# Reading a stored spectrum back in two loads per chunk instead of three (long convolution by FFT, then a phase MLP)

## The chip, the cores and the metric

One core of one Trainium2 chip runs the kernel. The metric is the device time of one execution in microseconds (us). Three runs of the kernel before gave 2083.17, 2084.01 and 2089.09 us; their median is 2084.01 us.

## What is computed

The reference has two parts. The change lies in the first.

```
Xf = rfft(x, n=2*S, axis=1);  Hf = rfft(h, n=2*S, axis=0)
y  = irfft(Xf * Hf, n=2*S, axis=1)[:, :S, :]        # x: 8 x 5696 x 128, h: 5696 x 128
theta = y @ w_theta;  zr, zi = y*cos(theta), y*sin(theta)
u = y + (w_tok_r @ zr + w_tok_i @ zi)               # over the 5696 tokens
out = u + relu(u @ w_ch)
```

The product `Xf * Hf` is complex: it needs, beside each part of x's spectrum, both the real and the imaginary part of h's.

## The kernel before, in words

**The transform.** A transform of length 11392 is cut into 178 x 64. Stage a (`stage_a`, matmuls L248) transforms along 178, of which the 90 frequencies 0 to 89 are kept; stage b (`stage_b`, whose matmuls are those of `f2`, L268) transforms along 64 and multiplies by h's spectrum; stages c (`stage_c`, L439 and L440) and d (`stage_d`, L475) go back. The work on x is cut into 8 groups: 4 pairs of batches times 2 halves of the 128 channels. A group passes all four stages.

**Stage b.** The 90 frequencies are walked in 12 chunks: 11 of 8 and a last one of 2. For a chunk, TensorE writes 64 real rows over 64 imaginary rows of x's spectrum into PSUM, ScalarE copies them to `xs` (L417; two buffers), and VectorE multiplies `xs` by both forms of h's spectrum in one instruction of 128 x 2048 (L419; the short last chunk takes two small ones, L424). The products go to `uv_t`, which stage c reads.

**The tile `hs`.** It holds, in 128 partitions, two rows of 512 f16 numbers (1 KB) each. Row 0 is "straight": the real part in partitions 0 to 63, the imaginary part in 64 to 127. Row 1 is "swapped": the imaginary part in 0 to 63, the real part in 64 to 127. There are four `hs` buffers (pool `fft_h`, L112). `load(c)` (L404 to L410) fills one: a load of 128 partitions for the straight row (L408), and two of 64 partitions for the swapped row (L410). Chunk c, once written down, calls `load(c + 4)` (L427), so a buffer that chunk c's multiply frees is refilled for chunk c + 4. Chunks 0 to 3 of the next group are loaded beside stage c.

**Where h's spectrum comes from.** At the start, h itself passes stages a and b. `h_chunk(c)` (L349) puts a chunk's result into the memory of `uv_t` (the views `hst`), and after every third chunk one store of 128 partitions (L362) writes three chunks to the HBM tensor `hf_hbm`. Four stores write all of it. The first multiply of group 0 writes to `uv_t` too, so it has to come after the stores have read their part of it.

**What sets the order.** VectorE, ScalarE and GpSimd (POOL) keep the order in which the code was written, by hand, until group 0 has passed stage c. The order on TensorE and on SyncE's queue (SP), which issues the stores L362 and the loads L408 and L410, is made by a planner. Each queue works in order: what waits at its head holds up what is behind. In one group's time, stage c of group g is woven with stage a of group g + 1 (L778), and then stage b of group g + 1 with stage d of group g (L786). Stage d evicts to `yt` by VectorE (L479) or ScalarE (L481), and at its end SP stores `yt` (L488). The inputs x of group g + 2 are fetched by POOL (L151) beside stage c. After the eight groups come the phases (sine and cosine) and the large product with `w_tok_r` and `w_tok_i` (L1187, L1266).

The pool's buffers serve for something else later: `phases_b` takes `hs` buffers in turn with others for its result `zz` (L582, L583).

Of the kernel before, what the change touches and what calls it, by code (L numbers as in the profile page):

```python
# [11 lines left out]
BF16 = mybir.dt.bfloat16  # L12
F16 = mybir.dt.float16
# [9 lines left out]
def kernel(  # L23
# [10 lines left out]
    nc = tc.nc  # L34
    B, S, D = x.shape
    assert D == 128
    P = 128
# [38 lines left out]
    N2 = 64  # L76
# [3 lines left out]
    CK = 8  # L80
    HD = D // 2
# [6 lines left out]
    NCK = len(CHK)  # L88
# [5 lines left out]
    RC = 2 * NP + 2 * ND  # L94
    M0, N0 = S // 4 // N2, S // 4 % N2
    assert S % 4 == 0 and S // 2 == NB // 2 * N2 + N2 // 2 and 2 * NP < N2 // 2
    hf_hbm = nc.dram_tensor("hf_hbm", (NCK, 2, P, HD * CK), F16, kind="Internal").ap()
    yt_hbm = nc.dram_tensor("yt_hbm", (D, B, S), BF16, kind="Internal").ap()

    psp = ExitStack()  # L100
# [2 lines left out]
    def psum():  # L103
        return fp.tile([P, 2, 512], F32, tag="ps", name="ps")

    conv, setup, xa, xin, pha = (ExitStack() for _ in range(5))

    def pool(name, bufs, stack, **kw):
        return stack.enter_context(tc.tile_pool(name=name, bufs=bufs, **kw))

    fa = pool("fft_a", 1, xa)
    fh = pool("fft_h", 4, xa)  # L112
    fx = pool("fft_x", 2, xin)
    NE, WB, BT = 9, 6 * 4 * CJ * 64, 7 * 1024
    keep = pool("keep", 1, ctx, side="right")
# [172 lines left out]
    hst = [t[:, :6 * D * CK].rearrange("p (c h d k) -> p c h d k", c=6, h=2, k=CK) for t in (u_t, v_t)]  # L288
# [60 lines left out]
    def h_chunk(c):  # L349
        c0, ck = CHK[c]  # L350
        ps = f2(a_h, c, 0)
        h_ = hst[c // 6][:, c % 6]
        dst = h_[:, :, :, :ck]
        if c in (0, 2, 5, 7, 10):
            nc.vector.tensor_scalar(dst, ps, 16.0 / NF, None, op0=mult)
        else:
            nc.scalar.activation(dst, ps, AF.Copy, scale=16.0 / NF)
        for cc, j in ((0, 0), (NCK - 1, CHK[-1][1] - 1)):
            if c == cc:
                nc.vector.tensor_scalar(dst[:, :, :, j], dst[:, :, :, j], 0.5, None, op0=mult)  # L360
        if c % 3 == 2:
            nc.sync.dma_start(  # L362
                hf_hbm[c - 2:c + 1].rearrange("c h p n -> p (c h) n"),
                hst[c // 6][:, c % 6 - 2:c % 6 + 1].rearrange("p c h d k -> p (c h) (d k)"))

    r_u = fc.tile([P, P], F16)
    r_v = fc.tile([P, RC], F16)
# [27 lines left out]
    def e_minus():  # L395
        nc.gpsimd.tensor_scalar(e_neg[:K1], e_t[:K1, 1:2 * NP:2], -1.0, None, op0=mult)

    LEAD = 4

    def stage_b(a_st, dh, warm=WARM):  # L400

        hs_of = {}

        def load(c):  # L404
            if c >= NCK:
                return
            hs = hs_of[c] = fh.tile([P, 2, HD * CK], F16, tag="hs", name="hs")
            nc.sync.dma_start(hs[:, 0], hf_hbm[c, dh])  # L408
            for e in range(2):
                nc.sync.dma_start(hs[64 * e:64 * e + 64, 1], hf_hbm[c, dh, 64 - 64 * e:128 - 64 * e])  # L410

        def chunk(c):
            c0, ck = CHK[c]
            hv = hs_of[c].rearrange("p r (d k) -> p r d k", k=CK)
            ps = f2(a_st, c, warm)
            xs = fs.tile([P, 2, HD, CK], F16, tag="xs", name="xs")
            nc.scalar.activation(xs[:, :, :, :ck], ps, AF.Copy)  # L417
            if ck == CK:
                nc.vector.tensor_tensor(  # L419
                    uv[:, :, :, c0:c0 + ck],  # L420
                    xs.rearrange("p e d k -> p e (d k)").unsqueeze(1).to_broadcast([P, 2, 2, HD * CK]),
                    hv.rearrange("p r d k -> p r (d k)").unsqueeze(2).to_broadcast([P, 2, 2, HD * CK]), op=mult)
            for r in range(2 if ck < CK else 0):
                nc.vector.tensor_tensor(  # L424
                    uv[:, 2 * r:2 * r + 2, :, c0:c0 + ck], xs[:, :, :, :ck],
                    hv[:, r:r + 1, :, :ck].to_broadcast([P, 2, HD, ck]), op=mult)
            load(c + LEAD)  # L427
        return [lambda c=c: load(c) for c in range(LEAD)], [lambda c=c: chunk(c) for c in range(NCK)]

# [63 lines left out]
    zz_n, ZB = [0], 3  # L493
# [11 lines left out]
    rr = []  # L505
    r_rest = [lambda: rr.extend([r_table(0, r_u), r_table(1, r_v)]), lambda: rr[0](), lambda: rr[1]()]
    h_chunk(0)
    w2_sine()
    w_rest(1)
    h_chunk(1)  # L510
    w2_cosine()
    for c in range(2, NCK):
# [24 lines left out]
    def phases_b(ti, y_ap, b0, nb, yT, sb, th_pool, th_tag, zi_eng, turns=None, tags=("red", "mag"), m=P,  # L537
                 theta_ps=None, copy=None, home={}):
        n = nb * D
        if theta_ps is None:  # L540
            theta_ps = th_pool.tile([P, n], F32, tag=th_tag, name="theta_ps")
        theta_ps = theta_ps[:m]
        y_ap = y_ap[:m]
        if tags is None:
            sin_, cos_ = (sb.tile([P, n], F16, tag=t, name=t)[:m] for t in ("sin", "cos"))
        else:
            red, mag = (sb.tile([P, n], F32, tag=t, name=t_)[:m] for t, t_ in zip(tags, ("red", "mag")))
            sin_, cos_ = (z.bitcast(F16)[:, :n] for z in (red, mag))
        if turns is None:
            for b in range(nb):  # L550
                nc.tensor.matmul(theta_ps[:, b * D:(b + 1) * D], yT[:, b, :],  # L551
                                 w_theta_sb, start=True, stop=True)
            nc.scalar.activation(red, theta_ps, AF.Identity, bias=magic[:m])  # L553
            nc.scalar.activation(mag, theta_ps, AF.Copy)
            nc.vector.scalar_tensor_tensor(red, red, MAGIC, mag,
                                           op0=ALU.subtract, op1=ALU.subtract)
            r = red
        else:
            mag = theta_ps
            ones, plus, minus, w_neg = turns  # L560
            for q in range(0, nb, 4):
                bank = theta_ps[:, q * D:(q + 4) * D]
                nc.tensor.matmul(bank, ones, plus, start=True, stop=False)
                for b in range(q, q + 4):
                    nc.tensor.matmul(theta_ps[:, b * D:(b + 1) * D], yT[:, b, :],
                                     w_theta_sb, start=False, stop=False)
                nc.tensor.matmul(bank, ones, minus, start=False, stop=False)
                for b in range(q, q + 4):
                    nc.tensor.matmul(theta_ps[:, b * D:(b + 1) * D], yT[:, b, :],
                                     w_neg, start=False, stop=(b == q + 3))  # L570
            r = theta_ps
        if copy is not None:
            copy()
        if turns is None:
            nc.scalar.activation(mag, r, AF.Abs)
        nc.scalar.activation(sin_, r, AF.Sin, bias=zero_b[:m], scale=-TWO_PI)
        if turns is not None:
            nc.scalar.activation(mag, r, AF.Abs)
        nc.scalar.activation(cos_, mag, AF.Sin, bias=half_pi[:m], scale=-TWO_PI)
        yflat = y_ap.rearrange("p b d -> p (b d)")  # L580
        if tags is None:
            k = zz_n[0] = (zz_n[0] + 1) % (4 + ZB)  # L582
            zz = (fh.tile([P, 2, HD * CK], F16, tag="hs", name="zz").bitcast(BF16) if k < 4 else  # L583
                  sides["phases"]["zz"].tile([P, 2, 512], BF16, tag="zz", name="zz"))
            zr, zi = zz[:, 0], zz[:, 1]
            sides["zz"] = zz
        else:
            zi, zr = (z.bitcast(BF16) for z in (sin_, cos_))
        zi_eng.tensor_mul(zi, sin_, yflat)
        nc.vector.tensor_mul(zr, cos_, yflat)  # L590
        cols = slice(b0 * D, b0 * D + n)
        q_ = b0 // 4
        for e in range((m + 63) // 64):
            rows = slice(e * 64, e * 64 + 64)
            if ti * P >= 2 * H:
                for r, z in enumerate((zr, zi)):
                    nc.sync.dma_start(zl_hbm[r, :, cols], z)
                continue
            p_, blk = divmod(2 * ti + e, 4 * NJ)
            i, j = divmod(blk, NJ)  # L600
            if tags is None and j in home:
                for r in range(2):
                    (nc.gpsimd if r else nc.sync).dma_start(
                        home[j][32 * i:32 * i + 32, :4096].rearrange("p (z q r n) -> p z q r n", z=2, q=2, r=2)[:, :, q_, r],
                        zz[e * 64 + r:e * 64 + 64:2])
            elif tags is None:
                nc.sync.dma_start(z_hbm[p_, j, q_, :, i].rearrange("z t n -> t z n"), zz[rows])
            else:
                for r, z in enumerate((zr, zi)):
                    nc.sync.dma_start(z_hbm[p_, j, q_, r, i], z[rows])  # L610
# [486 lines left out]
    for i, (k, p, tt, j0, s0, nj) in enumerate(stretches):  # L1097
# [38 lines left out]
        if tt is None:  # L1136
# [24 lines left out]
            if end_of_pair:  # L1161
# [5 lines left out]
                c, c0 = c_last  # L1167
# [161 lines left out]
```

## Time and profile before

| what | value |
|---|---|
| median of three runs | 2084.01 us |
| the profiled execution, its own time | 2084.83 us |
| its span, first to last instruction | 2083.0 us |
| TensorE busy (PE) | 1982.1 us, 95% |
| VectorE busy (DVE) | 1543.9 us, 74% |
| ScalarE busy (ACT) | 639.5 us, 31% |
| GpSimd busy (POOL) | 972.4 us, 47% |
| mean granted TensorE clock | 0.978 |
| multiplies L419: count, busy, mean | 88, 111.6 us, 1292 ns |
| loads of `hs`: 128 KB, 64 KB | 96 and 192 |
| stage b, first to last `hs` multiply of group 0 | 53.2 to 72.9 us |
| stage b, first to last `hs` multiply of group 7 | 356.1 to 379.0 us |

How to read it: PE is the matmuls, DVE is VectorE, ACT is ScalarE, SPq is SyncE's queue, where a row is the issue of one DMA. A line number such as L419 is the line of the kernel before. In the view of groups, a row gives busy time and mean duration, and behind the second bar the time that the engine sat idle just before these instructions, and what ended most of it. In the timeline, a row gives start and duration in us, and in brackets the idle time before it and what ended that. "Landing" is the time from a DMA's issue until its data is there.

### The profile page before, as it was taken

The numbers are of one execution on the slowest core, as the hardware profiler recorded it, in microseconds if no ns is written. First come the engines' busy times: TensorE is split into PE (matmuls) and PEld (weight loads), VectorE is DVE, ScalarE is ACT, GpSimd is POOL, SyncE is SP. The second block draws the span as 40 slices with busy tenths as digits, with TensorE's granted clock in tenths as the row PEclk, the third lists the DMA queues.
The fourth block names the chain that finished last, engine by engine and source line by source line (L and its number), as shares of the span: only waits on it lengthen the run. The fifth ranks groups of instructions, "written<-read, shape, count | busy, mean of one in ns | idle before, by whom it ended". The sixth has DMA issues, their size and how long they took to land.

```text
span 2083.0 us, 42942 instructions
## 1 busy us (share of the span) xinstructions
PE 1982.1 (95%) x16381; PEld 1098.0 (53%) x16381; DVE 1543.9 (74%) x2805; ACT 639.5 (31%) x936; POOL 972.4 (47%) x1770
## 2 busy tenths in 40 slices
PE   7698988889999999999999999899999999999998
PEld 5588888754444444444444444344444444444444
DVE  7867767666788787878777766876867777777767
ACT  6667777783333333333310000011111111111111
POOL 8432331247444454445566554445453545444450
PEclk9789999999999999999999999999999999999999
DMA  9699996999898999999999899879697878878793
GB/s 162 97 140 146 157 143 161 240 266 244 147 172 173 178 172 164 175 178 172 179 168 161 131 196 263 132 118 156 119 160 127 154 133 148 144 135 153 129 155 88
DMA packets 518014, 335.08 MB, mean 161 GB/s; under 512 B 186231, under 2 KB 483319, under 8 KB 516823
## 3 DMA queue, kind: packets, MB, share of 16 engines
q0 software_dynamic: 322368, 157.47, 60.0%
q1 hardware_dynamic: 189456, 163.34, 27.7%
q10 hardware_dynamic: 5984, 11.54, 1.6%
q8 instruction: 128, 2.10, 0.4%
q14 instruction: 78, 0.64, 0.1%
HBM read 376.39 MB, written 92.49 MB: 225 GB/s over the span
## 4 chain that ended last, share of the span: by engine, by line
PE 65%; DVE 3%; DMA 3%; issue 1%; POOL 1%; ACT 0%; DVEq 0%; ACTq 0%; SPq 0%
PE m L1266 60%; DVE b L822 1%; DVE c L1273 1%; DMA ring<-in_moe_w_tok_r_dram 1%; PE v L968 1%; PE utp L961 1%; PE m L1270 1%; DMA b<-z_hbm 1%; DVE wt L881 1%; POOL ring L667 1%; PE theta_ps L551 0%; PE tpz L909 0%; DMA wl<-in_moe_w_tok_i_dram 0%; PE m L1187 0%; PE m L1153 0%
## 5 line engine op out<-in xcount | busy, mean ns | idle before, releaser
L667 POOL DMA_DIRECT2D ring<-in_moe_w_tok_i_dram x720 | 387.9, 546 | 651.4 <-DVE wt L881 576.1
L667 POOL DMA_DIRECT2D ring<-in_moe_w_tok_r_dram x720 | 386.5, 547 | 151.0 <-DVE wt L881 82.7
L881 DVE STREAM_TRANSPOSE wt<-ring 128x384 f32<-128x384 f32 (+2 forms) x720 | 360.4, 527 | 120.1 <-PE m L1266 77.5
L1266 PE MATMUL m<-b,wt 128*128 128x512 bf16 x1640 | 390.1, 380 | 1.9 <-DVE wt L881 1.7
L1266 PEld LDWEIGHTS <-wt 128*128 128x128 bf16 x1804 | 176.3, 98 | 219.4 <-DVE wt L881 7.4
L1273 DVE TENSOR_TENSOR c<-c,m 128x512 f32<-128x512 f32 x412 | 266.9, 674 | 0.4 <-PE m L1266 0.4
L963 ACT ACTIVATE ring<-utp 128x512 bf16<-128x512 bf16 x85 | 50.7, 597 | 582.3 <-PE utp L961 582.3
L419 DVE TENSOR_TENSOR uv_t<-xs,hs 128x2048 f16<-128x2048 f16 x88 | 111.6, 1292 | 51.7 <-DMA hs<-hf_hbm 32.4
L439 PE MATMUL ps<-r_u,uv_t 128*128 128x128 f16 x1024 | 123.9, 226 | 16.1 <-DVE uv_t L424 10.9
L440 PE MATMUL ps<-r_v,uv_t 128*128 128x100 f16 x1024 | 121.4, 214 | 1.2 <-DVE uv_t L424 1.0
L1187 PE MATMUL m<-b,wt 128*128 128x512 bf16 x480 | 112.2, 383 | 6.4 <-DMA b<-zz 2.7
L958 ACT ACTIVATE ub<-c 128x512 bf16<-128x512 f32 x88 | 55.0, 628 | 191.8 <-DMA ring<-in_moe_w_tok_r_dram 113.2
L439 PEld LDWEIGHTS <-uv_t 128*128 128x128 f16 x1024 | 104.4, 102 | 12.5 <-DVE uv_t L424 12.1
L151 POOL DMA_DIRECT2D x<-in_x_dram x128 | 99.6, 785 | 22.8 <-POOL x L149 14.7
L440 PEld LDWEIGHTS <-uv_t 128*128 128x128 f16 x1024 | 103.9, 102 | 9.2 <-issue 6.2
L417 ACT ACTIVATE xs<-ps 128x1024 f16<-128x1024 f32 x96 | 91.7, 971 | 48.4 <-DVE uv_t L419 31.6
L1187 PEld LDWEIGHTS <-wt 128*128 128x128 bf16 x528 | 50.9, 99 | 66.4 <-issue 8.7
L268 PEld LDWEIGHTS <-w_t 64*128 64x128 f16 x3240 | 58.3, 99 | 43.8 <-issue 35.7
L553 ACT ACTIVATE red<-theta_ps,magic 128x512 f32<-128x512 f32 (+1 forms) x46 | 31.6, 687 | 155.3 <-PE theta_ps L551 89.4
L248 PE MATMUL ps<-f_t,x 89*128 89x180 f16 x512 | 66.0, 261 | 3.1 <-DVE a L255 1.4
L911 ACT ACTIVATE ring<-tpz 128x512 bf16<-128x512 bf16 (+1 forms) x46 | 27.5, 597 | 131.6 <-PE tpz L909 118.2
L822 DVE TENSOR_TENSOR b<-b 128x1024 bf16<-128x1024 bf16 x100 | 61.4, 684 | 0.0
(2924 smaller groups left out, 3774.6 us busy)
## 6 DMA issues: line engine op xcount, KB each, us to landing
ring<-in_moe_w_tok_r_dram POOLq DMA_DIRECT2D x352, 96.0 KB, 4.5
ring<-in_moe_w_tok_i_dram POOLq DMA_DIRECT2D x352, 96.0 KB, 5.0
ring<-in_moe_w_tok_r_dram POOLq DMA_DIRECT2D x352, 80.0 KB, 4.5
ring<-in_moe_w_tok_i_dram POOLq DMA_DIRECT2D x352, 80.0 KB, 3.9
cp_hbm<-c SPq DMA_DIRECT2D x88, 256.0 KB, 2.5
c<-cp_hbm SPq DMA_DIRECT2D x88, 256.0 KB, 4.3
out_dram<-c SPq DMA_DIRECT2D x88, 256.0 KB, 4.7
hs<-hf_hbm SPq DMA_DIRECT2D x96, 128.0 KB, 3.1
```

Of the source, the lines that this page charges most:

```text
L151: nc.gpsimd.dma_start(x16[p0:p1, e, n0:n0 + 16, :HD], bass.AP(tensor=src.tensor, offset=src.offset + (p0 * N2 + n0) * D + dh * HD, ap=[[N2 ...
L248: nc.tensor.matmul(ps[:, i // 2, (i % 2) * 2 * K1:(i % 2 + 1) * 2 * K1], lhs(q + i), f1_t[:NB], start=True, stop=True)
L417: nc.scalar.activation(xs[:, :, :, :ck], ps, AF.Copy)
L419: nc.vector.tensor_tensor(uv[:, :, :, c0:c0 + ck], xs.rearrange("p e d k -> p e (d k)").unsqueeze(1).to_broadcast([P, 2, 2, HD * CK]), hv. ...
L439: nc.tensor.matmul(o, u_t[:, at:at + P], r_u, start=True, stop=False)
L440: nc.tensor.matmul(o[:, 2 * NP:], v_t[:, at:at + P], r_v, start=False, stop=True)
L667: nc.gpsimd.dma_start(wb[32 * i:32 * i + 32, :ng, :nj * 64], bass.AP(tensor=a.tensor, offset=a.offset + row0 * S + p * H + i * QR + j0 * 6 ...
L822: return [lambda f=f, x=x: f(*x) for f, x in ((nc.vector.tensor_sub, (bt[M3], b12, b22)), (nc.vector.tensor_sub, (bt[M4], b21, b11)), (nc. ...
L881: nc.vector.transpose(wt.rearrange("p j t r -> p (j t r)").bitcast(F32).rearrange("p (j g t) -> p g j t", j=TJ, g=4)[:, :ng, :nj], wb[:, : ...
L1187: nc.tensor.matmul(ms[n // 2 * 2 + h], a[n][:, j, :, r], bts_of[p][jj][n % 2 * 2 + h][:, r, :], start=(n % 2 == 0 and jj == 0 and r == 0), ...
L1266: nc.tensor.matmul(ms[q], a[q][:, j, :, r], bts[jj][q][:, r, :], start=(jj == 0 and r == 0), stop=(jj == NJ - 1 and r == 1 and q not in left))
L1273: nc.vector.tensor_tensor(c, z, ms[q], op=op)
```

## The change

`hf_hbm` gets another shape. Before, a chunk and half of channels had 128 rows of 1 KB: 64 real, 64 imaginary. After, it has 64 rows of 2 KB, in which the real and the imaginary part of a row lie side by side. So partitions 0 to 63 of `hs` (real, imaginary) are one load of 64 rows as they lie, and partitions 64 to 127 (imaginary, real) are one load of the same 64 rows with the two parts in reverse order. A store of 128 partitions becomes two of 64, one for each part. `LEAD`, the number of buffers, stays 4 and only gets its name earlier.

```
-    hf_hbm = nc.dram_tensor("hf_hbm", (NCK, 2, P, HD * CK), F16, kind="Internal").ap()
+    hf_hbm = nc.dram_tensor("hf_hbm", (NCK, 2, N2, 2, HD * CK), F16, kind="Internal").ap()
...
+    LEAD = 4
...
-    fh = pool("fft_h", 4, xa)
+    fh = pool("fft_h", LEAD, xa)
...
-        if c % 3 == 2:
+        for ri in range(2 if c % 3 == 2 else 0):
             nc.sync.dma_start(
-                hf_hbm[c - 2:c + 1].rearrange("c h p n -> p (c h) n"),
-                hst[c // 6][:, c % 6 - 2:c % 6 + 1].rearrange("p c h d k -> p (c h) (d k)"))
+                hf_hbm[c - 2:c + 1, :, :, ri, :].rearrange("c h p n -> p (c h) n"),
+                hst[c // 6][64 * ri:64 * ri + 64, c % 6 - 2:c % 6 + 1].rearrange("p c h d k -> p (c h) (d k)"))
...
-            nc.sync.dma_start(hs[:, 0], hf_hbm[c, dh])
-            for e in range(2):
-                nc.sync.dma_start(hs[64 * e:64 * e + 64, 1], hf_hbm[c, dh, 64 - 64 * e:128 - 64 * e])
+            nc.sync.dma_start(hs[:64], hf_hbm[c, dh])
+            nc.sync.dma_start(hs[64:], hf_hbm[c, dh, :, ::-1, :])
...
-            k = zz_n[0] = (zz_n[0] + 1) % (4 + ZB)
-            zz = (fh.tile([P, 2, HD * CK], F16, tag="hs", name="zz").bitcast(BF16) if k < 4 else
+            k = zz_n[0] = (zz_n[0] + 1) % (LEAD + ZB)
+            zz = (fh.tile([P, 2, HD * CK], F16, tag="hs", name="zz").bitcast(BF16) if k < LEAD else
```

More of the change, by code (lines that the diff above doesn't have):

```diff
@@ L396, in e_minus @@
         nc.gpsimd.tensor_scalar(e_neg[:K1], e_t[:K1, 1:2 * NP:2], -1.0, None, op0=mult)
-    LEAD = 4
     def stage_b(a_st, dh, warm=WARM):
```

## The prediction, made before the changed kernel was run

> **What bounds the kernel now.** The chain of waits, followed back from the end, is TensorE nearly without a gap from about 600 us on; `hs` is not in it. So I read the first 380 us, where `hs` is used: the groups, SP's issues, VectorE's timeline, and the busy time by stage. The row of the multiply, and that of the 128 KB load:
>
> ```profile
> L419 DVE TENSOR_TENSOR uv_t<-xs,hs 128x2048 f16<-128x2048 f16 x88 | 111.6, 1292 | 51.7 <-DMA hs<-hf_hbm 32.4
> hs<-hf_hbm SPq DMA_DIRECT2D x96, 128.0 KB, 3.1
> ```
>
> VectorE sat idle for 51.7 us before L419, by most of it (32.4 us) for `hs`; four waits at L424 make it 34.6 us. Why is the data late, with four buffers? SP's issues in group 2:
>
> ```profile
> 147.09 0.33 SPq L408 DMA_DIRECT2D hs<-hf_hbm  x1
> 147.46 1.08 SPq L410 DMA_DIRECT2D hs<-hf_hbm  x2
> 148.64 0.53 SPq L408 DMA_DIRECT2D hs<-hf_hbm  x1
> 149.22 2.13 SPq L410 DMA_DIRECT2D hs<-hf_hbm  x2
> 151.45 0.53 SPq L408 DMA_DIRECT2D hs<-hf_hbm  x1
> 152.02 1.09 SPq L410 DMA_DIRECT2D hs<-hf_hbm  x2
> ```
>
> SP is never free here: one issue behind another takes 0.585 us, so three take 1.76 us a chunk. A multiply takes 1.226 us (the median of L419). SP, not the wires, is slower than VectorE. VectorE, same group:
>
> ```profile
> 149.11 2.35 DVE L419 TENSOR_TENSOR uv_t<-xs,hs 128x2048 f16<-128x2048 f16 x2
> 153.73 3.60 DVE L419 TENSOR_TENSOR uv_t<-xs,hs 128x2048 f16<-128x2048 f16 x3 [2.27 <-DMA hs<-hf_hbm]
> ...
> 160.16 2.41 DVE L419 TENSOR_TENSOR uv_t<-xs,hs 128x2048 f16<-128x2048 f16 x2 [0.71 <-DMA hs<-hf_hbm]
> 164.11 1.23 DVE L419 TENSOR_TENSOR uv_t<-xs,hs 128x2048 f16<-128x2048 f16 x1 [1.54 <-ACT yt L481]
> ```
>
> Chunk 4 (at 153.73) waits for a load whose last issue ended at 148.54: about 5 us, while x is still being fetched. The last line is chunk 10: its `xs` was done at 162.5 and its load's last issue ended at 161.21, so it too waited for `hs`, though the view names ScalarE. Matching chunks to loads in this way, I also count 2.22 and 1.15 us in group 3 and 0.56 us in group 6. In all the waits for `hs` are, by group 0 to 7: 7.9, 3.4, 4.5, 4.4, 4.5, 6.0, 4.2, 5.0, together 40 us.
>
> Do the stages have room? Busy time by stretch:
>
> ```profile
> 155.00:166.00 11.00, 7.84 (x182) 6.47 (x182) 8.68 (x9) 8.77 (x11) 0.00 (x0) 1.00 0.49 131
> 166.00:187.00 21.00, 20.93 (x388) 20.58 (x389) 14.26 (x12) 14.68 (x19) 9.44 (x18) 0.92 1.31 165
> ```
>
> The columns are the length, then PE, PEld, DVE, ACT and POOL busy, the clock, the DMA share and GB/s. Stage b (first row, its second half) leaves every engine idle at times, the DMA engines half of it. Stage c (second row) is TensorE's. So time won in stage b is won in the whole; time in stage c isn't touched.
>
> **The change, part by part.**
>
> *One issue less per chunk.* The built order of the instructions shows 192 loads instead of 288. On the three compute engines with a kept order nothing moves; TensorE shifts two and three neighbouring pairs. I take 0.585 us for an issue of either new form: 64-row issues of three dimensions (L607) have a median of 0.591 us, 64-row stores (L488) 0.568. Two take 1.17 us, under the multiply's 1.226, so SP stops setting the pace. After an idle SP the last issue of a chunk ends 0.95 us after the buffer is free, not 1.47 (0.33 + 1.08 and the gaps): 0.5 us earlier, and in a full queue another 0.59 us earlier with each chunk.
>
> What is late next: buffer free + 0.95 + landing against three further multiplies, 3.7 us. Late in a stage the data is there about 2.8 us after the last issue ends (161.21 to 164.1): 3.75, a near draw. Early in a stage, with x under way, it is 4 to 5 us, and only 0.5 us is won. So by group what stays is: 0: 1.6 (half of its first wait, below, and 0.5); 1: 2.7; 2 and 3: 1.7 each; 4: 0.7; 5: 1.0; 6: 0.3; 7: 3.6 (two waits beside the large loads of `ya`). Together 13; 27 us of 40 go.
>
> *What then takes the place.* In group 3, TensorE goes from 185.8 to 207.1, 21.3 us, with 18.3 us of work (360 matmuls L268 6.3, L475 8.9, L274 2.1, L248 1.0). It can give 3.0 us at the most, and its order ties it to ScalarE and VectorE. I pass on 0.63 of the 27 us: **17 us**. Bounds of this step: 0 and 40.
>
> *The stores.* Eight issues for four, 4 x 0.59 = 2.3 us more of SP, and they move: the built order has all eight ahead of the first load. Before, loads stood between them, waiting for the first store:
>
> ```profile
> 39.39 0.53 SPq L362 DMA_DIRECT2D hf_hbm<-uv_t  x1
> 39.96 0.55 SPq L408 DMA_DIRECT2D hs<-hf_hbm  x1
> 40.55 2.16 SPq L410 DMA_DIRECT2D hs<-hf_hbm  x2
> 42.81 0.67 SPq L362 DMA_DIRECT2D hf_hbm<-uv_t  x1
> ```
>
> The last store, ready at 37.9, went out at 42.8 and landed 10.2 us later, at 53.0. The first L419 began at 53.19, after 2.26 us idle: it writes the store's source, so this wait was for the store and not for a load. Now that store can go at about 38.5. VectorE's earlier work ends at 50.9, so up to 2.26 us are won. Against it, the stores compete earlier with x, and POOL's tables, for which VectorE waits until 48.27, stand behind x (it waits 1.95 and 2.36 us for landings). I take half, inside the 17. The first loads go about 1 to 2 us later than 37.45; nothing needs them before 50.9, 10 us later, which is their cover.
>
> *The rows.* Bytes stay, 256 KB a chunk. The trace has no load of 64 partitions with 128 KB and none in reverse order, so their landing is open: from 2.0 us (the least of any `hs` load) to 5.6 (`z_hbm<-zz`, the same shape the other way). In group 0 the 64 KB halves landed in 2.3 us, the full 128 KB in 2.4. I take no change; the step's bounds are in the range.
>
> [...]
>
> *The sum.* 2084.83 us (the profiled execution's own time, 0.8 above the median of the runs) less 17 is **2068 us**. Nothing else moves: the pool keeps its four buffers.
>
> **Rivals.**
>
> *Absorbed: 2082 us.* The waits go, but ScalarE's copies and TensorE come late instead. For it: stage b takes VectorE 20.0 to 20.4 us in groups 2, 3, 4 and 6, though their waits as the view names them differ from 1.1 to 4.5. Against it: by my matching the waits are alike (4.2 to 4.5), and the engines have 3 to 4 us idle in each. Only the start and some waits in groups 0 and 5 would be won, about 3 us.
>
> *The clock too: 2060 us.* After each stage b the granted clock drops: 0.72 in 166 to 172, then 1.00; likewise 0.72, 0.78, 0.72 and 0.76 for 6 us after groups 3 to 6. That costs 6 x (0.28 + 0.28 + 0.22 + 0.28 + 0.24) = 7.8 us. TensorE waits 1.4 to 2.6 us for the last multiply at that point, and if that goes, the drops may. [...] Against it: TensorE stays sparse in stage b's end in any case.
>
> *Slower: the reversed half-span load, 2103 us.* The place is the ring of four buffers. A buffer's round is a multiply, two issues and a landing, 1.23 + 0.95 + L, for four chunks. It equals today's 1.76 us a chunk at L = 4.9 us; beyond that the change loses. At L = 6 it is 2.05 a chunk, 0.28 more; with 8 refills in each of 8 groups 64 x 0.28 = 18 us. For it: the early loads already take 4 to 5 us, and a row of the same shape 5.6. Against it: 2.3 us in group 0.
>
> *It doesn't do what it says.* The built order shows it does, so this has no share.
>
> **Chances.** Forecast (10 to 25 us won) 0.50; with the clock 0.14; absorbed 0.20; slower 0.16. Runs of this kernel can tell about 0.3%, 6 us. Most of the absorbed case lies within that, and of the forecast a little: faster 0.67, same 0.18, slower 0.15. The range reaches from 2054, the clock case with the unknown landing at its best, to 2088, over the absorbed case and the mildest slower ones; about 0.1 is left out on each side.
>
> **What would show it.** Right: in stage b SP's issues come in pairs 1.17 us long with gaps between the pairs; the idle time for `hs` before L419 falls from 32.4 to near 13 us; the first L419 begins at 51 to 53 us; stage c's windows stay near 21 us; and group 7's last multiply ends some 17 us before 379. Wrong: a landing of `hs` above 4.9 us at the median; an issue of the reversed load above 1.17 us; or an unchanged stage b with idle time put down to `xs` and TensorE.

## The result, and the profile after

The changed kernel takes 2072.95 us (median of 4 runs, 2070.23 to 2073.84), the kernel before 2086.32 us (4 runs, 2083.17 to 2089.09): a ratio of 0.9934 with a 95% interval of 0.9914 to 0.9955, some 13 us. The forecast was 2068 us. Two later series, each beside runs of the kernel before, gave 0.9938 (0.9922 to 0.9953) and 0.9929 (0.9911 to 0.9946). The profiled execution took 2072.32 us, with a span of 2070.5 us.

First the group rows of the multiplies after the change (L417 was L419, L422 was L424; behind the last bar the idle time of VectorE and who ended it), then the row of the loads:

```profile
L417 DVE TENSOR_TENSOR uv_t<-xs,hs 128x2048 f16<-128x2048 f16 x88 | 110.5, 1290 | 40.7 <-DMA hs<-hf_hbm 22.3 <-ACT xs L415 18.2
L422 DVE TENSOR_TENSOR uv_t<-xs,hs 128x256 f16<-128x256 f16 x16 | 5.9, 410 | 11.0 <-ACT xs L415 10.8
```

```profile
hs<-hf_hbm SPq DMA_DIRECT2D x192, 128.0 KB, 3.6
```

Before, the row of the short last chunk was

```profile
L424 DVE TENSOR_TENSOR uv_t<-xs,hs 128x256 f16<-128x256 f16 x16 | 5.9, 395 | 5.0 <-ACT xs L417 2.8 <-DMA hs<-hf_hbm 2.2
```

The idle time for `hs` before both multiplies fell from 34.6 (32.4 + 2.2) to 22.3 us, not to 13. The wait of the short last chunk for `xs` grew from 2.8 to 10.8 us. SP's issues in group 2, and VectorE beside them:

```profile
144.34 0.45 SPq L407 DMA_DIRECT2D hs<-hf_hbm  x1
144.83 0.60 SPq L408 DMA_DIRECT2D hs<-hf_hbm  x1
...
149.38 0.60 SPq L408 DMA_DIRECT2D hs<-hf_hbm  x1
152.50 0.44 SPq L407 DMA_DIRECT2D hs<-hf_hbm  x1
...
155.55 0.54 SPq L407 DMA_DIRECT2D hs<-hf_hbm  x1
156.13 0.60 SPq L408 DMA_DIRECT2D hs<-hf_hbm  x1
157.00 0.44 SPq L407 DMA_DIRECT2D hs<-hf_hbm  x1
```

```profile
151.24 3.60 DVE L417 TENSOR_TENSOR uv_t<-xs,hs 128x2048 f16<-128x2048 f16 x3 [2.54 <-DMA hs<-hf_hbm]
...
155.76 4.73 DVE L417 TENSOR_TENSOR uv_t<-xs,hs 128x2048 f16<-128x2048 f16 x4
163.53 0.74 DVE L422 TENSOR_TENSOR uv_t<-xs,hs 128x256 f16<-128x256 f16 x2 [3.04 <-ACT xs L415]
```

A pair back to back takes 1.18 us (155.55 to 156.73, and in the median of all), and gaps stand between pairs: SP is idle from 149.98 to 152.50. The late waits for `hs` in this group are gone: four multiplies run without a gap from 155.76. But the fifth chunk, at 151.24, waits 2.54 us, where it waited 2.27 before. Its load's last issue ended at 145.43, 5.8 us earlier. And the last chunk waits 3.04 us for its `xs`. Why, ScalarE's and TensorE's rows tell:

```profile
163.08 0.42 ACT L415 ACTIVATE xs<-ps 128x256 f16<-128x256 f32 x1 [1.98 <-PE ps L275]
```

```profile
160.41 2.63 PE L275 MATMUL ps<-w_t 128*128 128x384 f16 x12
```

L275 are twelve filling matmuls, written before the last chunk's copy into the same PSUM tile and meant only to keep TensorE's clock up. The copy waits for them, 1.98 us. The clock (the figure ahead of the DMA share and the GB/s) in stage b of group 2, then in shorter stretches; the first two rows are the kernel before, its stage b and the first 6 us of the stage c behind it:

```profile
145.84:165.94 20.10, 15.97 (x484) 13.81 (x480) 15.57 (x15) 15.35 (x18) 3.52 (x6) 1.00 0.82 136
166.00:172.00 6.00, 6.00 (x79) 6.00 (x80) 3.64 (x3) 2.32 (x4) 1.11 (x2) 0.72 0.71 174
```

```profile
143.08:164.27 21.19, 18.22 (x484) 15.85 (x480) 15.57 (x15) 14.52 (x17) 3.53 (x6) 0.84 0.82 156
...
153.00:159.00 6.00, 4.72 (x112) 4.52 (x112) 5.97 (x6) 5.27 (x6) 0.00 (x0) 0.64 0.55 159
159.00:164.30 5.30, 5.25 (x53) 3.64 (x50) 2.22 (x4) 2.36 (x5) 0.00 (x0) 0.77 0.65 171
164.30:170.00 5.70, 5.68 (x100) 5.68 (x101) 3.65 (x4) 4.47 (x7) 1.88 (x4) 1.00 0.93 211
```

Before, the clock was 1.00 in this stage b and 0.72 in the first 6 us of the stage c behind it. Now it is low inside stage b, and stage c begins at 1.00. **The drop has moved.**

To add up, I cut the first part of the span at VectorE's timeline: stage b from a group's first to its last `hs` multiply, stage c (with what lies between) from there to the next group's first. "Clock lost" is the sum of (1 - clock) x length over groups 2 to 7. The last two columns are the later series of the changed kernel; of the kernel before there is one profile.

| us | before | after | after, 2nd | after, 3rd |
|---|---|---|---|---|
| first multiply begins | 53.2 | 53.1 | 54.0 | 53.5 |
| 8 stages b | 176.3 | 169.6 | 167.7 | 169.0 |
| 7 stages c | 149.5 | 141.8 | 146.0 | 142.3 |
| last multiply ends | 379.0 | 364.5 | 367.6 | 364.8 |
| from there to the end | 1704.0 | 1706.0 | 1707.0 | 1704.2 |
| clock lost in b | 5.6 | 12.1 | 10.1 | 10.1 |
| clock lost in c | 8.2 | 0.0 | 0.0 | 0.0 |

So the gain has two parts of like size: 6.7 to 8.6 us in stage b, and 3.5 to 7.7 us in stage c. What follows gives 0 to 3 us back; in all the profiles of this study that tail lies between 1702.4 and 1710.8 us, so I read no effect of the change in it.

### The profile page after: what moved, and what is told of

Same layout as the page of the kernel before. It is cut to its first block, busy times and chain, and to the rows that moved or that the text cites. A ratio compares the mean times of both kernels' runs of the same rounds, so it can differ in the third digit from the quotient of the medians.

```text
span 2070.5 us, 42579 instructions
## 1 busy us (share of the span) xinstructions
PE 1969.7 (95%) x16205; PEld 1094.1 (53%) x16381; DVE 1543.0 (75%) x2805; ACT 639.8 (31%) x936; POOL 976.6 (47%) x1770
## 4 chain that ended last, share of the span: by engine, by line
PE 65%; DVE 3%; DMA 3%; issue 1%; POOL 1%; ACT 0%; ACTq 0%; DVEq 0%
PE m L1264 61%; DMA b<-z_hbm 2%; DVE b L820 1%; DVE c L1271 1%; PE v L966 1%; PE utp L959 1%; PE m L1268 1%; POOL ring L665 1%; DVE wt L879 1%; PE theta_ps L549 0%; PE tpz L907 0%; DMA wl<-in_moe_w_tok_i_dram 0%; PE m L1151 0%; PE m L1185 0%; DMA ring<-in_moe_w_tok_i_dram 0%
## 5 line engine op out<-in xcount | busy, mean ns | idle before, releaser
L417 DVE TENSOR_TENSOR uv_t<-xs,hs 128x2048 f16<-128x2048 f16 x88 | 110.5, 1290 | 40.7 <-DMA hs<-hf_hbm 22.3
L437 PE MATMUL ps<-r_u,uv_t 128*128 128x128 f16 x1024 | 116.4, 219 | 5.5 <-ACT g__8966 L442 1.6
L438 PE MATMUL ps<-r_v,uv_t 128*128 128x100 f16 x1024 | 114.0, 207 | 0.4
L415 ACT ACTIVATE xs<-ps 128x1024 f16<-128x1024 f32 x96 | 91.6, 972 | 51.5 <-DVE uv_t L417 26.5
L438 PEld LDWEIGHTS <-uv_t 128*128 128x128 f16 x1024 | 99.9, 98 | 8.4 <-issue 6.5
L437 PEld LDWEIGHTS <-uv_t 128*128 128x128 f16 x1024 | 100.0, 98 | 0.9 <-DVE uv_t L422 0.3
```

The source lines that it names most:

```text
L417: nc.vector.tensor_tensor(uv[:, :, :, c0:c0 + ck], xs.rearrange("p e d k -> p e (d k)").unsqueeze(1).to_broadcast([P, 2, 2, HD * CK]), hv. ...
L437: nc.tensor.matmul(o, u_t[:, at:at + P], r_u, start=True, stop=False)
L438: nc.tensor.matmul(o[:, 2 * NP:], v_t[:, at:at + P], r_v, start=False, stop=True)
```

## The experiments

Theory after the result: SP's work per chunk sets stage b (**A**). Rivals: the landing of half-span loads (**B**); the filling matmuls (**C**); where the clock falls. The kernels ran in three groups, each on one chip, beside runs of the kernel before.

### Three loads again, from the new rows

```
-            nc.sync.dma_start(hs[64:], hf_hbm[c, dh, :, ::-1, :])
+            for r in range(2):
+                nc.sync.dma_start(hs[64:, r], hf_hbm[c, dh, :, 1 - r, :])
```

> The kernel after with the reversed load cut into its two parts, so three issues per chunk again, same bytes, same stores, same tensor in HBM. Theory A (the number of issues on SP sets how late hs is): SP's issues run back to back at 1.76 us a chunk in stage b, the waits of VectorE for hs return to above 30 us, and the time to within 4 us of the kernel before. Theory B (the wider rows or the fewer and larger DMAs land sooner, the issues don't matter): at least two thirds of the gain stay, 9 us or more below the kernel before.

Measured: 2092.87 us (2091.12 to 2100.59), ratio 1.0045 (1.0029 to 1.0061): slower than the kernel before, by 8 us, where theory A allowed 4. Its SP rows in group 2, and its multiply:

```profile
151.26 1.62 SPq L409 DMA_DIRECT2D hs<-hf_hbm  x2
152.98 0.54 SPq L407 DMA_DIRECT2D hs<-hf_hbm  x1
153.57 1.24 SPq L409 DMA_DIRECT2D hs<-hf_hbm  x2
155.08 0.45 SPq L407 DMA_DIRECT2D hs<-hf_hbm  x1
```

```profile
L418 DVE TENSOR_TENSOR uv_t<-xs,hs 128x2048 f16<-128x2048 f16 x88 | 111.9, 1292 | 59.3 <-DMA hs<-hf_hbm 42.2 <-ACT xs L416 16.9
```

SP is full again: a chunk's three issues take 1.83 us (152.98 to 154.81) and more, where they took 1.76 before; all three are now 64-row loads. The waits for `hs` are 43.5 us with L423's, the stages b 184.1. The landing stayed low, 3.2 us for the 128 KB loads and 2.8 for the 64 KB ones, and yet the time was worst. That is for A and against B as the main cause. The clock goes with it: the stages c are back at 151.5 us, with 9.7 us of clock lost in them. The profiled execution was the slowest of the six, 2100.59 us, so its waits and stages are on the high side.

### The old rows, two loads

The kernel before with its four stores and its HBM shape, and two loads that pick the parts out as 1 KB pieces.

```
-            nc.sync.dma_start(hs[:, 0], hf_hbm[c, dh])
-            for e in range(2):
-                nc.sync.dma_start(hs[64 * e:64 * e + 64, 1], hf_hbm[c, dh, 64 - 64 * e:128 - 64 * e])
+            rows = hf_hbm[c, dh].rearrange("(r p) n -> p r n", r=2)
+            nc.sync.dma_start(hs[:64], rows)
+            nc.sync.dma_start(hs[64:], rows[:, ::-1, :])
```

> The kernel before with its tensor and its four stores as they were, and two loads per chunk: each takes 64 rows of two 1 KB pieces, the second with the pieces in reverse order. Theory A: stage b is as in the kernel after; at the start the loads stand between the stores again, as before, and the first multiply waits 2.3 us instead of 3.2; in all 0 to 2 us faster than the kernel after. Theory B (the 2 KB rows side by side matter): the landing rises by 0.5 us or more and the time is 4 us or more above the kernel after.

Measured: 2070.17 us (2065.15 to 2078.07), ratio 0.9934 (0.9916 to 0.9952), the changed kernel's. The gain comes from the count of the loads. The layout in HBM and the eight stores add nothing to it that can be measured, nor do they cost: the first multiply began at 52.8 us here, with four stores, and between 51.5 and 54.0 in the profiles with eight.

### Neither load reversed, and both reversed

```
-            nc.sync.dma_start(hs[64:], hf_hbm[c, dh, :, ::-1, :])
+            nc.sync.dma_start(hs[64:], hf_hbm[c, dh])
```

> The kernel after with the second load in straight order too; partitions 64 to 127 get the real and the imaginary part in the wrong places, so the result isn't the reference's. Theory A: the order of the two 1 KB parts costs nothing, the time is that of the kernel after within 4 us, an issue stays near 0.59 us and the landing near 3.6 us. Rival (the reversed load, with 1 KB pieces, is what lands later than hoped): the landing falls by 0.5 us or more and the time by 5 us or more below the kernel after.

Measured: 2065.23 us (2065.01 to 2066.18), ratio 0.9909 (0.9895 to 0.9923). Pace of a pair 1.17 us, landing 3.5. This is some 4 to 6 us below the changed kernel's three ratios, with intervals that overlap a little. Hence its counterpart, with `::-1` on both:

```
-            nc.sync.dma_start(hs[:64], hf_hbm[c, dh])
+            nc.sync.dma_start(hs[:64], hf_hbm[c, dh, :, ::-1, :])
```

> The changed kernel with both loads in reverse order: partitions 0 to 63 get their two parts in each other's place (the output is another one). The number of issues stays. It doubles the suspected cost of the reverse order, 1 KB pieces in place of 2 KB ones, of which the kernel with neither load reversed showed up to 5 us. If the pieces cost that, 2077 to 2081 us, an issue pair of 1.25 to 1.35 us or a landing above 3.7 us. If not, 2070 to 2076 us, the changed kernel's time.

Beside it ran the changed kernel as it is:

> The changed kernel as it is, beside the others on the same chip: 2070 to 2076 us, ratio 0.993 to 0.995.

Measured: both reversed 2073.81 us (2069.00 to 2075.89), ratio 0.9925 (0.9906 to 0.9944); the changed kernel 2073.53 us (2069.88 to 2076.26), ratio 0.9929 (0.9911 to 0.9946). A second reversed load cost nothing, though the pair took 1.22 us. That alone doesn't clear the first: a chunk waits for the later of its two loads. But the waits for `hs` before the full multiplies are 22.8 us with no load reversed, 24.2 with both, and 21.5 to 26.5 in the three profiles of the changed kernel, so they show no effect of the order. The price of the reverse order is not shown: one pair of kernels has 5 us, the other none. In its profile the kernel without it had stages b of 166.4 us (1.3 to 3.2 below the changed kernel's) and the shortest tail of all, 1702.4 us; that part can have nothing to do with the loads. I leave it open.

### The filling matmuls

The kernel before with 8 more of them in the stages b of groups 1 to 7 (12 to 20), meant to take its clock drops away without touching the loads:

```
-        return (steps, *stage_b(a_st, dh, WARM if g else WARM // 2))
+        return (steps, *stage_b(a_st, dh, WARM + 8 if g else WARM // 2))
```

> The kernel before, loads and all, with 8 more idle matmuls (20 for 12) behind the last chunk of stage b in groups 1 to 7, 1.3 us at the full clock. If the drops of the granted clock at the start of stage c come from TensorE's gap before its first matmul there, they go without any change to the loads: stage c's windows fall from 21.3 to 21.5 us to about 19.9 and the time by 5 to 8 us. If they come from all of stage b's thin second half, the drops stay, and the time is unchanged or up to 9 us longer (7 x 1.3).

Measured: 2085.41 us (2079.90 to 2089.18), ratio 1.0007 (0.9994 to 1.0020). Its stages c fell from 149.5 to 146.0 us, its stages b rose from 176.3 to 179.7. A part of stage c's time is to be had without the loads, but not for nothing. The changed kernel with 6 and with none:

```
+        return (steps, *stage_b(a_st, dh, WARM // 2))
...
+        return (steps, *stage_b(a_st, dh, 0 if g else WARM // 2))
```

> The kernel after with 6 idle matmuls instead of 12 behind the last chunk of stage b in groups 1 to 7. In the kernel after the last chunk's copy to xs waits for these matmuls, since they write the same PSUM tile (waits of 0.8 to 4.1 us before the last multiplies). Theory (what is late next is this fill): the wait before the last multiplies falls by about 1 us in each group, 5 to 8 us faster than the kernel after. Rival (without them the granted clock drops at the start of stage c again): stage c goes back to 21.3 us in most groups and the time is the same or up to 6 us longer.

> The kernel after with no idle matmuls behind the last chunk in groups 1 to 7. Theory (the fill is what is late next, and TensorE is dense enough without it): 8 to 15 us faster than the kernel after. Rival (the clock needs it): stages c of 21 us and more, and a time the same as or longer than with 6.

and, for comparison in the same group, the changed kernel once more:

> The kernel after itself, as the yardstick for the three runs beside it on this chip: 11 to 16 us below the kernel before. Its stage b and stage c lengths also tell which parts of the first profile repeat: if the gain is mostly the clock in stage c, at least five of the six stages c of groups 2 to 7 are again 19.9 us long; if it is mostly stage b, stage b's lengths in groups 3 to 6 are again 1 to 3 us below those of the kernel before.

Measured: with 6, 2076.07 us (2074.10 to 2076.95), ratio 0.9946 (0.9931 to 0.9961); with none, 2067.95 us (2064.17 to 2073.70), ratio 0.9911 (0.9892 to 0.9929); the changed kernel, 2074.86 us (2069.97 to 2076.34). The last chunk's row with none:

```profile
L422 DVE TENSOR_TENSOR uv_t<-xs,hs 128x256 f16<-128x256 f16 x16 | 5.7, 397 | 2.5 <-DMA hs<-hf_hbm 1.6 <-ACT xs L415 1.0
```

The wait for `xs` falls from 10.8 (8.3 in the profile beside it) to 1.0 us, and 6 to 7 us of the time go, by intervals of the ratio that still overlap: three of the six runs took 2064 to 2065 us, the others 2071 to 2074. With 6 matmuls it falls too, to 0.7, and the time does not: a miss. Its stages b of groups 2 to 7 were 4.3 us shorter than the control's, but the profiled tail was 1710.8 us. So C may be a part, of some 6 us, and it isn't a steady one.

### One load per chunk

```
-            nc.sync.dma_start(hs[:64], hf_hbm[c, dh])
-            nc.sync.dma_start(hs[64:], hf_hbm[c, dh, :, ::-1, :])
+            nc.sync.dma_start(hs, hf_hbm[c].rearrange("h p r n -> (h p) r n"))
```

> The kernel after with one load per chunk: 128 rows of 2 KB, 256 KB in one DMA. It takes the rows of both halves of channels instead of the two orders of one, so the result isn't the reference's. SP needs 0.6 us a chunk. If the pace of SP still limits the kernel after, this is 6 us or more faster than it; if what is left is the landing of the early loads beside x and the engines themselves, it is 0 to 5 us faster, and the waits for hs of chunk 4 in groups 2 to 5 are still 0.5 to 2 us.

Measured: 2061.67 us (2057.17 to 2063.14), ratio 0.9882 (0.9863 to 0.9900): 13 us below the changed kernel.

```profile
L416 DVE TENSOR_TENSOR uv_t<-xs,hs 128x2048 f16<-128x2048 f16 x88 | 110.4, 1290 | 30.6 <-ACT xs L414 23.6 <-DMA hs<-hf_hbm 6.8
```

```profile
hs<-hf_hbm SPq DMA_DIRECT2D x96, 256.0 KB, 3.7
```

An issue takes 0.32 us (median), and 256 KB land in 3.7 us, no later than 128 KB did. The waits fall to 6.8 us, the stages b to 158.6 (in the fastest of the four executions, 2057.17 us). Part of the 13 us could lie in the order, since nothing is reversed here either: against the two straight loads, measured on another chip, it is some 6 us by the ratios. The waits for `hs`, 6.8 us against 22.8 with two straight loads, speak for the single load itself. **My view that two issues under the multiply's 1.23 us take SP out of the matter is refuted**: what a chunk needs of SP and of loads still counted.

### One load per chunk, from a second copy

From group 2 on, `hf_hbm` has a second, swapped copy. ScalarE's queue makes it beside stage b of group 1, in 8 DMAs from HBM to HBM.

```
+            if g > 1:
+                nc.sync.dma_start(hs, hf_hbm[c, dh].rearrange("s p r n -> (s p) r n"))
+                return
...
+            copied = nc.scalar.activation(xs[:, :, :, :ck], ps, AF.Copy).ins
+            if g == 1 and c == 1:
+                with tc.issue_after(copied):
+                    for q in range(0, NCK, 3):
+                        for r in range(2):
+                            nc.scalar.dma_start(hf_hbm[q:q + 3, :, 1, :, r].rearrange("c h p n -> p (c h) n"),
+                                                hf_hbm[q:q + 3, :, 0, :, 1 - r].rearrange("c h p n -> p (c h) n"))
```

> The changed kernel, but from group 2 on each chunk comes in one load of 128 partitions. For that a second, swapped copy of h's spectrum is written in HBM by 8 DMAs (3 MB) that ScalarE's queue issues beside stage b of group 1; groups 0 and 1 load as after the change. All that is computed stays. Theory (SP's pace per chunk and not the landing sets stage b): groups 2 to 7 win what the kernel with one wrong load won, 13 us times 6/8, about 9 or 10 us against the changed kernel; from it goes what the copy takes from group 1, up to 5 us. So 2063 to 2070 us, and loads of 256 KB that land in 3.5 to 4 us. Rival (the copy holds up ScalarE's queue or group 1's loads, or the gain of the one load came from its reading the same rows for both halves less often): the changed kernel's time or up to 10 us above, with stage b of group 1 over 22 us or idle time for hs in groups 2 to 7 like after the change.

Measured: 2061.52 us (2060.65 to 2062.43), ratio 0.9872 (0.9853 to 0.9891), 12 us below the changed kernel on the same chip (2073.53) and just under the 2063 to 2070 expected. It beats both kernels. Its multiply's group row, then stage b of groups 2 and 7 by windows; the last line is the changed kernel's group 7:

```profile
L426 DVE TENSOR_TENSOR uv_t<-xs,hs 128x2048 f16<-128x2048 f16 x88 | 110.6, 1291 | 31.9 <-ACT xs L418 19.8 <-DMA hs<-hf_hbm 11.8
```

```profile
142.46:161.25 18.79, 15.73 (x484) 13.71 (x480) 15.57 (x15) 14.41 (x17) 3.52 (x6) 1.00 0.91 168
...
333.10:351.24 18.14, 15.82 (x487) 13.76 (x485) 15.72 (x15) 14.12 (x16) 2.18 (x4) 1.00 0.81 271
```

```profile
338.96:364.46 25.50, 20.60 (x487) 17.36 (x485) 15.72 (x15) 14.24 (x16) 2.53 (x4) 0.73 0.75 218
```

Group 7's stage b is 7.4 us shorter with the same work (487 matmuls), which costs TensorE 15.8 us at a clock of 1.00 and 20.6 at 0.73. That is the largest of three such differences: in the other two profiles of the changed kernel this stage took 24.1 and 22.4 us, at 0.79 and 0.85. Its last multiply ends at 351.2 us, 13.5 before the control's, and all but 0.1 of that lies in stage b (155.6 against 169.0; stage c 142.6 against 142.3, the start 0.5 earlier). The clock lost in stage b of groups 2 to 7 is 1.8 us, against 10.1. So late data and a slower TensorE go together in these profiles; whether the first brings the second is not shown.

The copy did hold up ScalarE:

```profile
92.54 14.44 ACTq L423 DMA_DIRECT2D hf_hbm<-hf_hbm  x7
107.08 1.94 ACT L418 ACTIVATE xs<-ps 128x1024 f16<-128x1024 f32 x2 [13.54 <-DMA hs<-hf_hbm]
```

Its queue was held for 14.44 us, and for 13.54 us no copy of `xs` was made; VectorE waited 6.22 us for one. Yet stage b of group 1 took 29.9 us, no longer than in the changed kernel (30.3 to 33.0): the rival's mechanism was there, and the length of this stage doesn't show it. Last, with no filling matmuls as well:

```
+        return (steps, *stage_b(a_st, dh, 0 if g else WARM // 2, g))
```

> As the kernel with the second copy, and with no filling matmuls in stage b from group 1 on (0 for WARM). All that is computed stays. If the two gains are of different kinds (late data; xs late behind the filling matmuls), they add: another 4 to 6 us, 2058 to 2065 us. If both are the same slack, which the last engine to be late takes back, the time is that of the kernel with the second copy, within 2 us.

Measured: 2063.21 us (2061.68 to 2063.80), ratio 0.9879 (0.9860 to 0.9898). Nothing more is won. The wait of the last chunk for `xs` falls from 6.6 to 0.4 us, that of the others for `xs` rises from 19.8 to 27.4. It fits that the filling matmuls and the late data share one slack, which whatever is late last takes. But the clock is a rival: without the filling matmuls 6.8 us of it were lost in stage b of groups 2 to 7, against 1.8 with them, and group 7 ran at 0.76 in place of 1.00. These runs don't separate the two.

## Why the prediction was right, and where it was off

**The bound and the direction: right.** The loads that SP issues per chunk decided, as the series shows: three from the new rows 2092.9, three as before 2084.6 to 2087.3, two 2070 to 2075 (2065 with none reversed, 2068 without the filling matmuls), one 2062 us.

**The pace: right.** Pairs of 1.18 us with gaps between them, against 1.17. After an idle SP, though, I took 0.95 us for a pair, and it was 1.09 (144.34 to 145.43).

**The waits that go: mis-sized, and this is the step that failed.** I let 27 of 40 us go and 13 stay. In the profiles 21.5 to 26.5 us stay and 8 to 13 go (of the 34.6 that the view names). Late in a stage the forecast held; early it did not. The fifth chunk of a group shows it, in means over groups 2 to 7 from SP's and VectorE's timelines:

| us | three loads (before) | two (three profiles) | one (both halves of channels; second copy) |
|---|---|---|---|
| group's first multiply begins, to end of the chunk's last issue | 2.8 | 2.6, 2.3, 2.6 | 1.6, 1.6 |
| from there to the chunk's multiply | 4.3 | 4.6, 5.0, 4.5 | 4.8, 4.8 |
| its wait | 1.5 | 1.5, 1.7, 1.4 | 0.7, 0.7 |

I let 0.5 us of this wait go, and none went. In group 2 the chunk's last issue ends only 0.36 us sooner behind the first multiply (2.35 for 2.71 us), and the multiply comes 0.6 us later behind that issue (5.8 for 5.2), where I had costed 4 to 5. The two loads of 64 rows also landed later than the old straight one: 3.6 us in the median where I took 3.1.

**The share passed on: about right.** I took 0.63, bounded by the 3.0 us that TensorE can give and not derived further. Three loads as before against one (34.6 to 6.8 us of waits, 176.3 to 158.6 us of stage b): 17.7 / 27.8 = 0.64. For the change itself it scatters: 6.7 / 12.3 = 0.54 in the first profile, 8.6 / 8.1 = 1.06 and 7.3 / 13.1 = 0.56 in the others. With the right size of the waits, 12.3 x 0.63 = 7.7 us, stage b would have come out as it did, 6.7 to 8.6.

**"Time in stage c isn't touched": wrong, and it made good most of what was missing.** Stage c won 3.5 to 7.7 us. This was my rival "the clock too", priced at 7.8; I had it on top of the 17, it came in place of the missing 9. So the mechanism in stage b was right, but that the total came within 5 us of the forecast was in part luck: a gain that I had put at nothing stood in for one that I had put too high. All of the clock lost in stage c went (8.2 to 0.0), but 4.5 to 6.5 us more were lost in stage b, where the slack covers some of it. In the second profile stage c won only 3.5 us with its clock at 1.00: in three of its seven stages TensorE stood still once, for 1.2 to 1.4 us, waiting for nothing that the profile names. The three profiles of the changed kernel have group 5 at 0.91, 1.00 and 0.83 in stage b, and group 2 at 0.84 in all: the same code got the same clock in one group and another one each time in the other. Why the drops come earlier now is not shown.

**The stores: wrong.** I costed an issue at 0.59 us and half of 2.26 us won.

```profile
30.73 12.85 SPq L363 DMA_DIRECT2D hf_hbm<-uv_t  x8
43.67 1.10 SPq L407 DMA_DIRECT2D hs<-hf_hbm  x1
```

Eight issues took SP from 30.73 to 43.58, 1.46 us each in the median. The last store went out at about 42, not at 38.5, and the first load of `hs` at 43.7, 6 us later than before where I had allowed 1 to 2. Now the first multiply waits 3.23 us for `hs`, where it waited 2.26 for the store, and begins at 53.1 as before. Four stores with two loads begin at 52.8, and the other profiles with eight stores at 51.5 to 54.0. So the order of stores and loads did not set the start; that it is the amount of data under way with x is my guess, and no run took x away.

**The rows: near my value.** I took no change. The landing rose by 0.5 us for the same 128 KB (3.1 us in the median for 128 partitions, 3.6 for the two loads of 64); with three loads a chunk from the new rows, the one of 64 partitions and 128 KB took 3.2. And 128 partitions took in 256 KB in 3.7 us, about what 64 needed for half of it. All of this was far from the 4.9 us of my slower rival. The single load has two things in its favour, a shorter issue on SP (0.32 us against 1.18 for a pair) and twice the bytes in a landing of like length. For the fifth chunk the table above tells them apart: the issue ends 0.8 to 1.0 us sooner, while the time from there to the multiply is no shorter than with two loads (4.8 against 4.5 to 5.0). For the rest of the 12 us it stays open.

**Absorbed, and slower: not seen.** The new waits for `xs` (10.8 us at L422) are the beginning of the first, and most of them went when the filling matmuls were left out, with some 6 us of the time in one pair of kernels and nothing in another.

## What to carry to other kernels

When a small load is late, count what each chunk costs its issuing queue and compare that with the consumer's time; but being just under it (1.18 against 1.23 us here) is not the end: one load in place of two was worth about as much again as two in place of three (12 to 13 us; 6 to 8 by the ratios if the kernel with neither load reversed is the yardstick). Size the waits that stay by the landing in the same stretch, not by the median, and ask whether an engine that waits will also lose its clock (in group 7 the same matmuls cost TensorE 20.6 us at a clock of 0.73 with two loads a chunk, 15.8 at 1.00 with one). Look at the stage behind for the second half of a gain.

## What the runs showed of the hardware that I had not expected

- After an idle SP, one issue took 0.32 us (median) for 256 KB to 128 partitions, and 0.45 for the first of two loads of 128 KB to 64 partitions; the second, right behind it, took 0.60. The larger load was the cheaper one to issue, and landed about as soon (3.7 against 3.6 us).
- Eight stores of 384 KB held SP for 12.85 us, 0.57 to 2.70 us an issue, where the four stores of 768 KB before took 0.36 to 0.67 us each. Eight copies from HBM to HBM kept ScalarE's queue, and with it ScalarE, for 14 to 15 us, although their issues took only 4.6 us in all; the rest lies between them, and what they waited for is not shown.
- Twelve filling matmuls, meant to keep the clock up, became what the last chunk waited for. In group 2 of the changed kernel they took 2.63 us, with the clock at 0.77 in that stretch, and the chunk waited 3.04 us; in the kernel before, with the clock at 1.00, they took 2.12 us; and with one load per chunk, the clock at 1.00 in that stage b, the chunk still waited 2.06.
